# One ring of four PSUM banks for gate, value, attention and W products in a fused attention and SwiGLU kernel

## The chip, the core and the metric

The kernel runs on one core of a Trainium2 chip. The metric is the device time of one execution in microseconds (us). A measurement here can tell two kernels apart when they differ by about 0.2%, which is 1.5 us. In what follows PE is the matrix engine (TensorE), DVE the vector engine, ACT the scalar engine, POOL GpSimd, and SP the engine that issues most DMAs.

## The reference

Eight batches of eight heads with 576 positions of 64 elements go through an attention in two stages: 32 learned queries `p` first gather from all 576 positions, and all positions then attend to these 32 packed rows. The result is the input of a SwiGLU layer of width 512 with a hidden width of 1536.

```python
p_packed = sm_attn(p, k, v)               # (8, 8, 32, 64)
out = sm_attn(q, p_packed, p_packed)      # (8, 8, 576, 64)
x = attn_out.transpose(0, 2, 1, 3).reshape(8 * 576, 512)
g = x @ w_gate                            # 512 x 1536
silu = g * (1.0 / (1.0 + np.exp(-g)))
return silu * (x @ w_val) @ w_out         # 1536 x 512
```

## The kernel before

**What is multiplied.** Since the second attention reads only 32 packed rows for each head, the kernel multiplies these rows with the gate and value weights first: for a batch it forms products M of the packed rows (`ppt`) and the weights (`w_s`), and then multiplies M with the attention weights of the 576 positions (`a2h`, `a2l`). Each operand is kept as a high and a low part, so that a product is three passes: `ml` with `a2h`, `mh` with `a2l`, `mh` with `a2h`.

**Steps.** After a start phase that handles batch 0 (to about 118 us), `batch(1)` follows (118 to 205 us) and then `batch2(b)` for b = 2 to 7. The hidden width is cut into 12 steps, `fc` = 0 to 11. In `batch2` a step is, in the order of PE: chunk A (gate, then value, of 256 or 320 columns: two PSUM banks, called A0 and A1 below, `chunk`, L1248), then `half(0)` (the first half of the products with the output weights for an earlier step, `products`, L1180, in the `acc` banks), chunk B (two banks, B0 and B1), then `half(1)`. ACT reads the gate bank (silu, `sg`, L1254), and DVE then reads the value bank (the product with `sg`, L1261, and for a B chunk a small one into `t`, L1264). Batch 1 has the same chunks in `gv_chunk` (L694, silu L701).

**What runs between the chunks.** After the value matmuls of a chunk a callback `fill` runs with a count that goes from 1 to 8 over the step (two in each chunk, two in each half). At count 2 of each odd step, right behind A1, `m_part` puts two more banks of products on PE, M0 and M1 (32 x 512 each on a part of the array, by a helper, L285 `aux<-w_s,ppt`). ACT rounds them into `mh` (L658), and then DVE makes `ml` (L603), which is the last reader of M0 and M1.

The attention for batch b + 1 is spread over batch b by a table of words, where "1.ha" stands for step 1, in front of `half(0)`. Those that take PSUM banks for PE are `q0` in step 11 of the batch before and `q1` in step 1 (`q_scores`, two banks, L425 `gv_aux<-k_t,p_t`, whose readers are DVE L440 and L441 in `q_read`), `pack` in step 5 (one bank, L509, whose reader is DVE L521 with the result `ppt`), and `mm0` and `mm1` in steps 7 and 9 (two banks each). All of them come right behind A1 or the M products and ahead of `half(0)`. So q0 and q1 stand between A1 and B0 in the order of banks.

In the even batches, step 0 also multiplies the hidden columns that the two batches of a pair share (`p4_step`, six of them, L713 `aux<-t_parts`). All six add into one bank, which `emit_out` copies to `ot` for the DMA to `out` (DVE L193).

**Banks.** Of the eight PSUM banks four are `acc`. Two are `ps_gv`, for the chunks and the attention's scores and packs (`gv_ps`), and two are `ps_aux`, for M and `p4_step` (`ps`). A bank is given again to a later tile when all readers of the tile in it are done, and the first matmul into it waits for that.

**What sets the order.** PE's order is that of the program, by hand. On DVE and ACT a scheduler of the framework orders the instructions, with the attention's kept in program order among themselves (`pin`).

Of the kernel before, what the change touches and what calls it, by code (L numbers as in the profile page):

```python
# [10 lines left out]
F32 = mybir.dt.float32  # L11
# [8 lines left out]
PSUM = bass.MemoryType.PSUM  # L20
# [5 lines left out]
P = 128  # L26
# [107 lines left out]
def tile_pack_attention_swiglu(ctx: ExitStack, tc: tile.TileContext, qT, q0, kT, v, vq, pT, wgv, wout, out):  # L134
# [5 lines left out]
    pool = ctx.enter_context(tc.tile_pool(name="pool", bufs=1))  # L140
    dram = ctx.enter_context(tc.tile_pool(name="dram", bufs=1, space=DRAM))
    ps_acc = ctx.enter_context(tc.tile_pool(name="ps_acc", bufs=4, space=PSUM))
    ps_gv = ctx.enter_context(tc.tile_pool(name="ps_gv", bufs=2, space=PSUM))
    ps_aux = ctx.enter_context(tc.tile_pool(name="ps_aux", bufs=2, space=PSUM))

    early_stack = ExitStack()
    early = early_stack.enter_context(tc.tile_pool(name="early", bufs=1))
# [29 lines left out]
    def pin(ins):  # L177

        return tc.keep_in_program_order(ins) if steady[0] else ins

    def ps():
        turn[0] += 1
        if wide[0] and turn[0] % 2:
            return ps_acc.tile([P, 512], F32, tag="acc", name="acc_aux")
        if wide[0]:
            return ps_gv.tile([P, 512], F32, tag="gv", name="gv_aux")
        return ps_aux.tile([P, 512], F32, tag="aux", name="aux")
# [217 lines left out]
    sq, sc = {}, {}  # L405

    def gv_ps():
        return ps_gv.tile([P, 512], F32, tag="gv", name="gv_aux")

    def q_scores(b, g, bank=ps):  # L410

# [196 lines left out]
    def store_w(k):  # L608
        nc.sync.dma_start(wd[k], w_t[k].rearrange("p h f n -> p (h f n)"))
# [52 lines left out]
    def m_part(b, k, fcs):  # L662
        m_mm(b, k, fcs)
        m_high(b, k, fcs)
# [15 lines left out]
    def gv_chunk(b, fc, is_b, fill, behind, between):  # L680
        odd = b % 2
        n = NB if is_b else NA
        off = (0 if odd else 256) if is_b else (320 if odd else 0)
        mh, ml = ms[b, fc // 2]
        ah, al = a2[b]
        f = fc % 2
        pgs = []
        for s in range(2):
            pg = ps_gv.tile([P, 512], F32, tag="gv", name="gv")
            pgs.append(pg)  # L690
            i = 0
            for m_, a_ in ((ml, ah), (mh, al), (mh, ah)):
                for g in range(NPAR):
                    nc.tensor.matmul(  # L694
                        pg[:, :n], m_[:, g, f, s * P : (s + 1) * P], a_[:, g, off : off + n],
                        start=(i == 0), stop=(i == 5),
                    )
                    i += 1
            fill()
        sg = pool.tile([P, NB], F32, tag="sg", bufs=1, name="sg")  # L700
        nc.scalar.activation(sg[:, :n], pgs[0][:, :n], AF.Silu)  # L701
        behind()
        hf = early.tile([P, 256], F32, tag="hf", bufs=2, name="hf")
        o, o4 = (64, 0) if is_b and odd else (0, 256)
        nc.vector.tensor_tensor(hf, pgs[1][:, o : o + 256], sg[:, o : o + 256], op=ALU.mult)
        if is_b:
            r, r4 = slice(64 * odd, 64 * odd + 64), slice(o4, o4 + 64)
            nc.vector.tensor_tensor(t4[b // 2][:, fc, r], pgs[1][:, r4], sg[:, r4], op=ALU.mult)
        return h_split(hf, nc.scalar, nc.vector, between)
# [82 lines left out]
    with tc.manual_schedule(engines={mybir.EngineType.PE}):  # L792
# [315 lines left out]

        for k in range(NFC // 2):
            store_w(k)  # L1110
        batch(1, behind)
        early_stack.close()
        late = ctx.enter_context(tc.tile_pool(name="late", bufs=1, reuse_waits="tile"))
# [122 lines left out]
        def chunk(b, fc, is_b, fill, behind):  # L1236
            odd = b % 2
            n = NB if is_b else NA
            off = (0 if odd else 256) if is_b else (320 if odd else 0)
            mh, ml = ms[b, fc // 2]  # L1240
            ah, al = a2[b]
            pgs = []
            for s in range(2):
                pg = ps_gv.tile([P, 512], F32, tag="gv", name="gv")
                pgs.append(pg)
                todo = [(m_, a_, g) for m_, a_ in ((ml, ah), (mh, al), (mh, ah)) for g in range(NPAR)]
                for i, (m_, a_, g) in enumerate(todo):
                    nc.tensor.matmul(  # L1248
                        pg[:, :n], m_[:, g, fc % 2, s * P : (s + 1) * P], a_[:, g, off : off + n],
                        start=(i == 0), stop=(i == 5),  # L1250
                    )
                fill()
            sg = pool.tile([P, NB], F32, tag="sg", bufs=1, name="sg")
            nc.scalar.activation(sg[:, :n], pgs[0][:, :n], AF.Silu)  # L1254
            behind()
            at = b, int(is_b), fc // 2
            if fc % 2 == 0:
                raw[at] = places.pop(0)
            x = raw[at][:, fc % 2].rearrange("p t n -> p (t n)")
            o, o4 = (64, 0) if is_b and odd else (0, 256)  # L1260
            nc.vector.tensor_tensor(x, pgs[1][:, o : o + 256], sg[:, o : o + 256], op=ALU.mult)  # L1261
            if is_b:
                r, r4 = slice(64 * odd, 64 * odd + 64), slice(o4, o4 + 64)
                nc.vector.tensor_tensor(t4[b // 2][:, fc, r], pgs[1][:, r4], sg[:, r4], op=ALU.mult)  # L1264

        def batch2(b):
            if not b % 2:
                t4_of(b)
            run = plan_of(b)
            for fc in range(NFC):  # L1270
                t = (b - 2) * NFC + fc
                cur, nxt = pair_at(t), pair_at(t + 1)
                tail = b % 2 == 0 and fc == 0
                count, step = [0], [0]

                def fill():
                    count[0] += 1
                    if count[0] == 2:
                        run(fc, 2)
                        if fc == NFC - 1 and b + 1 < B:  # L1280
                            m_part(b + 1, 0, both)
                            load_ws(b + 1, 1)
                        elif fc % 2 and fc + 1 < NFC:
                            k = (fc + 1) // 2
                            m_part(b, k, both)
                            load_ws(*((b, k + 1) if k < 5 else (b + 1, 0)))
                    else:
                        run(fc, count[0])
                    if tail and count[0] in (1, 3, 4, 5, 6, 8):
                        p4_step(step[0], b - 1)  # L1290
                        step[0] += 1

                def half(which):
                    if cur:
                        products(cur, which, fill)
                    else:
                        fill(), fill()

                chunk(b, fc, False, fill, lambda: run(fc, "a"))
                run(fc, "ha")  # L1300
                if cur:
                    split_sums(cur)
                m_lows()
                half(0)
                if nxt:
                    split_raw(nxt)
                    sum_raw(nxt)
                chunk(b, fc, True, fill, lambda: run(fc, "b"))
                run(fc, "hb")
                half(1)  # L1310
# [56 lines left out]
```

## Time and profile before

| | before |
|---|---|
| median of 3 runs | 752.55 us (752.15 to 753.63) |
| profiled execution, its own time | 754.22 us |
| its span in the trace | 752.4 us |
| mean granted TensorE clock | 0.995 |
| PE busy | 712.0 us (95%) |
| DVE busy | 503.7 us (67%) |
| ACT busy | 403.8 us (54%) |
| POOL busy | 137.6 us (18%) |

The span goes from the first to the last instruction of the trace, and 1.8 us of the profiled execution's time lie around it. Busy time of PE includes the filling of its pipeline, because the ends of matmuls are modelled; a loss of time on PE is better read from the distance between the starts of two instructions. A note in square brackets at a row's end is the idle time ahead of it and what ended that.

### The profile page before, as it was taken

The numbers are of one execution on the slowest core, as the hardware profiler recorded it, in microseconds if no ns is written. First come the engines' busy times: TensorE is split into PE (matmuls) and PEld (weight loads), VectorE is DVE, ScalarE is ACT, GpSimd is POOL, SyncE is SP. The second block draws the span as 40 slices with busy tenths as digits, with TensorE's granted clock in tenths as the row PEclk, the third lists the DMA queues.
The fourth block names the chain that finished last, engine by engine and source line by source line (L and its number), as shares of the span: only waits on it lengthen the run. The fifth ranks groups of instructions, "written<-read, shape, count | busy, mean of one in ns | idle before, by whom it ended". The sixth has DMA issues, their size and how long they took to land.

```text
span 752.4 us, 16344 instructions
## 1 busy us (share of the span) xinstructions
PE 712.0 (95%) x6503; PEld 617.4 (82%) x6503; DVE 503.7 (67%) x1123; ACT 403.8 (54%) x714; POOL 137.6 (18%) x301
## 2 busy tenths in 40 slices
PE   7999988999988998999989999999998999999995
PEld 5777776888876887989879888889887898989985
DVE  4986896767845676677655676676745767646453
ACT  3888455635635465735626357554644546444432
POOL 0000000000010031322303223232311322232331
PEclk9999999999999999999999999999999999999998
DMA  9999953031232433334223342344314322310001
GB/s 356 341 350 349 326 209 124 3 128 64 78 140 91 183 123 128 135 127 166 95 104 120 128 149 111 142 134 144 122 54 155 110 91 113 141 57 29 2 29 42
DMA packets 25436, 103.27 MB, mean 137 GB/s; under 512 B 6672, under 2 KB 7952, under 8 KB 16656
## 3 DMA queue, kind: packets, MB, share of 16 engines
q1 hardware_dynamic: 25072, 102.00, 37.0%
q8 instruction: 51, 0.84, 0.5%
q10 hardware_dynamic: 288, 0.23, 0.1%
q14 instruction: 25, 0.20, 0.1%
HBM read 86.44 MB, written 15.78 MB: 136 GB/s over the span
## 4 chain that ended last, share of the span: by engine, by line
PE 77%; DVE 12%; ACT 5%; issue 2%; DMA 2%; POOL 1%; ACTq 0%; DVEq 0%; SPq 0%; POOLq 0%
PE gv L1248 29%; PE acc L1180 20%; PE acc L713 7%; PE aux L285 6%; PE gv L694 5%; PE gv L944 3%; PE aux L713 3%; DVE ml L603 2%; PE gv_aux L285 1%; DVE ppt L521 1%; DVE ot L1210 1%; ACT mh L658 1%; DMA out<-ot 1%; PE warm_ps L799 1%; ACT sg L1254 1%
## 5 line engine op out<-in xcount | busy, mean ns | idle before, releaser
L1248 PE MATMUL gv<-a2h,ml 128*128 128x256 f32 (+1 forms) x576 | 129.2, 305 | 19.4 <-DVE e L441 8.5
L1248 PE MATMUL gv<-a2l,mh 128*128 128x256 f32 (+1 forms) x576 | 122.1, 293 | 0.0
L1248 PE MATMUL gv<-a2h,mh 128*128 128x256 f32 (+1 forms) x576 | 122.0, 293 | 0.0
L1248 PEld LDWEIGHTS gv<-a2h,ml 128*128 128x128 f32 x576 | 90.0, 188 | 31.0 <-ACT sg L1254 10.5
L1248 PEld LDWEIGHTS gv<-a2l,mh 128*128 128x128 f32 x576 | 91.8, 188 | 0.0
L1248 PEld LDWEIGHTS gv<-a2h,mh 128*128 128x128 f32 x576 | 91.8, 188 | 0.0
L1254 ACT ACTIVATE sg<-gv 128x256 f32<-128x256 f32 (+1 forms) x144 | 59.3, 412 | 51.7 <-PE gv L1248 42.8
L603 DVE TENSOR_TENSOR ml<-aux,mh 128x512 fp32r<-128x512 f32 (+1 forms) x94 | 60.6, 676 | 34.9 <-ACT mh L658 34.8
L1154 ACT CAST hs<-s_raw 128x384 fp32r<-128x384 f32 x72 | 37.0, 514 | 79.3 <-PE acc L1180 76.7
L658 ACT CAST mh<-aux 128x512 fp32r<-128x512 f32 (+1 forms) x94 | 50.0, 584 | 46.9 <-PE aux L285 46.2
L1180 PE MATMUL acc<-wo_h,ho 128*128 128x256 f32 x288 | 66.5, 293 | 2.3 <-DVE ho L1133 2.1
L1180 PEld LDWEIGHTS acc<-wo_h,ho 128*128 128x128 f32 x288 | 49.1, 188 | 18.3 <-issue 14.8
L1180 PE MATMUL acc<-t_w,hs 128*128 128x256 f32 x432 | 62.8, 280 | 0.0
L1180 PE MATMUL acc<-t_w,ho 128*128 128x256 f32 x432 | 62.5, 279 | 0.0
L1180 PEld LDWEIGHTS acc<-t_w,hs 128*128 128x128 f32 x432 | 58.2, 188 | 0.8 <-DVE ot L1210 0.2
L1180 PEld LDWEIGHTS acc<-t_w,ho 128*128 128x128 f32 x432 | 56.1, 188 | 0.2
L1133 DVE TENSOR_TENSOR hs<-s_raw,hs 128x384 fp32r<-128x384 f32 x72 | 39.7, 551 | 21.0 <-ACT hs L1154 20.1
L1139 POOL TENSOR_TENSOR s_raw<-extra 128x128 f32<-128x128 f32 x36 | 16.7, 465 | 196.0 <-DVE hs L1133 177.7
L1261 DVE TENSOR_TENSOR more<-gv,sg 128x256 f32<-128x256 f32 x72 | 30.2, 420 | 27.3 <-PE gv L1248 27.0
L1139 POOL TENSOR_TENSOR s_raw<-more 128x128 f32<-128x128 f32 x36 | 16.6, 462 | 167.3 <-DVE hs L1133 167.3
L1261 DVE TENSOR_TENSOR extra<-gv,sg 128x256 f32<-128x256 f32 x72 | 30.3, 420 | 22.9 <-PE gv L1248 18.9
L285 PE MATMUL aux<-w_s,ppt 64*32 64x512 f32 x576 | 41.3, 601 | 2.3 <-DVE ot L193 2.3
(221 smaller groups left out, 1531.1 us busy)
## 6 DMA issues: line engine op xcount, KB each, us to landing
w_s<-wd SPq DMA_DIRECT2D x36, 1024.0 KB, 5.2
st<-in_wgv SPq DMA_DIRECT2D x12, 1024.0 KB, 7.6
k_t<-in_kT SPq DMA_DIRECT2D x16, 576.0 KB, 4.9
out<-ot SPq DMA_DIRECT2D x35, 256.0 KB, 2.3
q_t<-in_qT SPq DMA_DIRECT2D x14, 576.0 KB, 6.6
v_t<-in_vq SPq DMA_DIRECT2D x6, 1280.0 KB, 8.2
st<-in_wout SPq DMA_DIRECT2D x6, 1024.0 KB, 7.3
wd<-w SPq DMA_DIRECT2D x6, 1024.0 KB, 12.6
```

What stands on the lines that cost most here:

```text
L285: nc.tensor.matmul(outs[par][32 * hp : 32 * hp + 32], lhs(r, hp), rhs(r, hp), start=True, stop=True)
L603: pin(nc.vector.tensor_tensor(*x[1], op=ALU.subtract))
L658: nc.scalar.copy(m[0][at], src)
L694: nc.tensor.matmul(pg[:, :n], m_[:, g, f, s * P : (s + 1) * P], a_[:, g, off : off + n], start=(i == 0), stop=(i == 5),)
L713: nc.tensor.matmul(acc[:, at], h_[:, c : c + P], w_[fc // 2][:, fc % 2, at], start=((fc == 0 or first) and i == 0), stop=(fc == NFC - 1 an ...
L1133: nc.vector.tensor_tensor(dst, src, high.bitcast(F32), op=ALU.subtract)
L1139: nc.gpsimd.tensor_tensor(s_raw[:, 0], a21, a11, op=ALU.subtract)
L1154: nc.scalar.copy(hi, s_raw)
L1180: nc.tensor.matmul(acc[bank][:, QC * col : QC * col + QC], h_[:, x], w_, start=(k == 0 and i == 0 and col == 0), stop=(k == 5 and i == 2 a ...
L1248: nc.tensor.matmul(pg[:, :n], m_[:, g, fc % 2, s * P : (s + 1) * P], a_[:, g, off : off + n], start=(i == 0), stop=(i == 5),)
L1254: nc.scalar.activation(sg[:, :n], pgs[0][:, :n], AF.Silu)
L1261: nc.vector.tensor_tensor(x, pgs[1][:, o : o + 256], sg[:, o : o + 256], op=ALU.mult)
```

## The change

The pools `ps_gv` and `ps_aux` are closed after the start phase, and one pool of four banks takes their place from `batch(1)` on. The chunks, the attention's tiles, M and `p4_step` all take the next bank of it in program order. Where nothing holds a bank for long, a tile follows the one four allocations back. `p4_step` holds its bank over step 0 and a part of step 1 of an even batch, and there the other three rotate. The six steps of `p4_step` stand at counts 2 to 7 rather than 1, 3, 4, 5, 6 and 8.

```diff
-    ps_gv = ctx.enter_context(tc.tile_pool(name="ps_gv", bufs=2, space=PSUM))
-    ps_aux = ctx.enter_context(tc.tile_pool(name="ps_aux", bufs=2, space=PSUM))
+    narrow_stack = ExitStack()
+    ps_gv = narrow_stack.enter_context(tc.tile_pool(name="ps_gv", bufs=2, space=PSUM))
+    ps_aux = narrow_stack.enter_context(tc.tile_pool(name="ps_aux", bufs=2, space=PSUM))
+    ring = []
...
+    def ring_ps(name):
+        return ring[0].tile([P, 512], F32, tag="ring", name=name)
+
     def ps():
+        if ring:
+            return ring_ps("aux")
...
     def gv_ps():
-        return ps_gv.tile([P, 512], F32, tag="gv", name="gv_aux")
+        return ring_ps("gv_aux") if ring else ps_gv.tile([P, 512], F32, tag="gv", name="gv_aux")
...
-            pg = ps_gv.tile([P, 512], F32, tag="gv", name="gv")
+            pg = ring_ps("gv")
...
+        narrow_stack.close()
+        ring.append(ctx.enter_context(tc.tile_pool(name="ps_ring", bufs=4, space=PSUM, reuse_waits="tile")))
         batch(1, behind)
...
-                pg = ps_gv.tile([P, 512], F32, tag="gv", name="gv")
+                pg = ring_ps("gv")
...
-                    if tail and count[0] in (1, 3, 4, 5, 6, 8):
+                    if tail and 1 < count[0] < 8:
```

The lines of the changed kernel lie 7 further down from L425 on (L432), and 9 from L1180 on (L1189). PE's instructions are the same, and one of the `p4_step` moves in each of the batches 2, 4 and 6 from between A0 and A1 to behind A1. On ACT eight instructions change places and on DVE 21, with none added; what changes at most places is only which bank is waited for.

Step 11 of batch 4, in PE's order before. A0 and A1 are `gv_5600` and `gv_5610`, M0 and M1 `aux_5619` and `aux_5620`, the two banks of q0 `gv_aux_5639` and `gv_aux_5640`, B0 and B1 `gv_5685` and `gv_5692`.

```order
L1248 MATMUL gv_5600<-a2h_4063,ml_5441 128x256 [waits Activation_49]
...
L1248 MATMUL gv_5610<-a2h_4063,ml_5441 128x256 [waits DVE_49,PE_49]
...
L285 MATMUL aux_5619<-w_s_5454,ppt_5106 32x512 [waits DMAHW3_49]
L285 MATMUL aux_5620<-w_s_5454,ppt_5106 32x512
...
L425 MATMUL gv_aux_5639<-k_t_4952,p_t_4950 32x144 [waits DMAHW4_49,Activation_49]
L425 MATMUL gv_aux_5640<-k_t_4952,p_t_4950 32x144 [waits DVE_49]
...
L1248 MATMUL gv_5685<-a2h_4063,ml_5441 128x320 [waits DVE_49,PE_49]
...
L1248 MATMUL gv_5692<-a2h_4063,ml_5441 128x320 [waits Activation_49]
```

The two banks of the chunks go round as A0, A1, q0, q0, B0, B1, so B0 comes into the bank that q0's first tile has just filled, and B1 into the one of the second. The same place after the change, with A0 and A1 as `gv_5605` and `gv_5615`:

```order
L1257 MATMUL gv_5605<-a2h_4068,ml_5446 128x256 [waits Activation_49]
...
L1257 MATMUL gv_5615<-a2h_4068,ml_5446 128x256 [waits DVE_49]
...
L292 MATMUL aux_5624<-w_s_5459,ppt_5111 32x512 [waits DMAHW3_49,Activation_49]
L292 MATMUL aux_5625<-w_s_5459,ppt_5111 32x512 [waits DVE_49,PE_49]
...
L432 MATMUL gv_aux_5644<-k_t_4957,p_t_4955 32x144 [waits DMAHW4_49,Activation_49]
L432 MATMUL gv_aux_5645<-k_t_4957,p_t_4955 32x144 [waits DVE_49]
...
L1257 MATMUL gv_5690<-a2h_4068,ml_5446 128x320 [waits DVE_49]
...
L1257 MATMUL gv_5697<-a2h_4068,ml_5446 128x320 [waits DVE_49]
```

The four banks go round as A0, A1, M0, M1, then q0 in those of A0 and A1, and B0 and B1 in those of M0 and M1. B0 and B1 now wait for DVE's `ml` of M0 and M1.

Step 1 of batch 4, in PE's order before, where M0 and M1 are `aux_4692` and `aux_4693`, the tiles of q1 `gv_aux_4709` and `gv_aux_4710`, B0 and B1 `gv_4759` and `gv_4766`:

```order
L285 MATMUL aux_4692<-w_s_4461,ppt_3936 32x512 [waits DMAHW0_49]
L285 MATMUL aux_4693<-w_s_4461,ppt_3936 32x512 [waits DVE_49]
...
L425 MATMUL gv_aux_4709<-k_t_3782,p_t_3780 32x144 [waits Activation_49]
L425 MATMUL gv_aux_4710<-k_t_3782,p_t_3780 32x144
...
L1248 MATMUL gv_4759<-a2h_4063,ml_4448 128x320 [waits DVE_49,PE_49]
...
L1248 MATMUL gv_4766<-a2h_4063,ml_4448 128x320 [waits Activation_49]
```

And after, the same tiles as `aux_4697`, `aux_4698`, `gv_aux_4714`, `gv_aux_4715`, `gv_4764` and `gv_4771`:

```order
L292 MATMUL aux_4697<-w_s_4466,ppt_3941 32x512 [waits DMAHW0_49,DVE_49,PE_49]
L292 MATMUL aux_4698<-w_s_4466,ppt_3941 32x512 [waits Activation_49]
...
L432 MATMUL gv_aux_4714<-k_t_3787,p_t_3785 32x144 [waits DVE_49]
L432 MATMUL gv_aux_4715<-k_t_3787,p_t_3785 32x144 [waits DVE_49]
...
L1257 MATMUL gv_4764<-a2h_4068,ml_4453 128x320 [waits DVE_49]
...
L1257 MATMUL gv_4771<-a2h_4068,ml_4453 128x320 [waits DVE_49]
```

Before, M1 came into the bank of `p4_step`, and its first matmul waited for DVE's copy of that bank (L193). After, `p4_step` still holds a bank here, so three rotate: M1 comes into A0's bank, q1's first tile into A1's, its second into M0's, B0 into M1's. The wait of `gv_aux_4715` is for DVE's `ml` of M0.

DVE's order at the same place, before (`ot_4665<-aux_4552` is the copy of `p4_step`'s bank, `extra` the product of A1):

```order
L1261 TENSOR_TENSOR extra_2495<-gv_4683,sg_4706 128x256 [waits PE_49,Activation_49]
L193 COPY ot_4665<-aux_4552 128x512 [waits DMAHW1_49,DVE_49]
L603 TENSOR_TENSOR ml_4691<-aux_4692,mh_4690 128x512 [waits Activation_49]
L603 TENSOR_TENSOR ml_4691<-aux_4693,mh_4690 128x512 [waits Activation_49]
L440 TENSOR_REDUCE z1_4467<-gv_aux_4709 128x2 [waits PE_49]
```

And after:

```order
L1270 TENSOR_TENSOR extra_2500<-gv_4688,sg_4711 128x256 [waits PE_49,Activation_49]
L610 TENSOR_TENSOR ml_4696<-aux_4697,mh_4695 128x512 [waits Activation_49]
L610 TENSOR_TENSOR ml_4696<-aux_4698,mh_4695 128x512 [waits Activation_49]
L200 COPY ot_4664<-aux_4564 128x512 [waits DMAHW1_49,DVE_49]
L447 TENSOR_REDUCE z1_4472<-gv_aux_4714 128x2 [waits PE_49]
```

The copy with its wait for a DMA has moved behind the two `ml`.

## Rows read from the trace of the kernel before

**Rows 1.** The page's busy times, and its groups by line (part 5)

```profile
PE 712.0 (95%) x6503; PEld 617.4 (82%) x6503; DVE 503.7 (67%) x1123; ACT 403.8 (54%) x714; POOL 137.6 (18%) x301
...
L1248 PE MATMUL gv<-a2h,ml 128*128 128x256 f32 (+1 forms) x576 | 129.2, 305 | 19.4 <-DVE e L441 8.5
...
L1248 PE MATMUL gv<-a2h,mh 128*128 128x256 f32 (+1 forms) x576 | 122.0, 293 | 0.0
```

**Rows 2.** Busy time by stretch, batch 5: length, PE, PEld, DVE, ACT, POOL, clock, DMA, GB/s

```profile
464.00:555.00 91.00, 87.43 (x854) 78.51 (x854) 62.75 (x145) 53.75 (x91) 24.95 (x53) 1.00 0.35 124
```

**Rows 3.** Waits of PE from 160 us on: total us, times, longest us

```profile
PE gv L1248 <- DVE e L441: 8.5, 9, 2.8
PE gv L1248 <- ACT sg L1254: 7.5, 11, 1.6
PE aux L285 <- DVE ot L193: 2.3, 2, 1.2
...
PE gv L1248 <- DVE ppt L521: 1.5, 4, 0.4
```

**Rows 4.** Timeline of PE around step 11 of batch 4 (start, length)

```profile
458.89 1.09 PE L285 MATMUL aux<-w_s,ppt 64*32 64x512 f32 x16
...
460.45 0.39 PE L1180 MATMUL acc<-wo_h,ho 128*128 128x256 f32 x1
...
461.28 0.86 PE L1180 MATMUL acc<-t_w,ho 128*128 128x256 f32 x6
462.98 0.53 PE L1248 MATMUL gv<-a2h,ml 128*128 128x320 f32 x2 [0.84 <-DVE e L441]
...
464.69 0.57 PE L1248 MATMUL gv<-a2h,ml 128*128 128x320 f32 x2 [0.59 <-ACT sg L1254]
...
465.69 0.86 PE L1180 MATMUL acc<-t_w,hs 128*128 128x256 f32 x6
...
468.81 0.87 PE L1180 MATMUL acc<-t_w,ho 128*128 128x256 f32 x6
...
471.27 0.87 PE L1180 MATMUL acc<-t_w,hs 128*128 128x256 f32 x6
```

**Rows 5.** Timeline of DVE at the same place

```profile
460.69 1.29 DVE L603 TENSOR_TENSOR ml<-aux,mh 128x512 fp32r<-128x512 f32 x2 [1.20 <-ACT mh L658]
```

**Rows 6.** Timeline of PE, step 1 of batch 4

```profile
387.35 1.04 PE L285 MATMUL aux<-w_s,ppt 64*32 64x512 f32 x2
...
391.09 0.39 PE L1180 MATMUL acc<-wo_h,ho 128*128 128x256 f32 x1
...
396.25 0.87 PE L1180 MATMUL acc<-t_w,hs 128*128 128x256 f32 x6
```

**Rows 7.** Timeline of DVE, step 1 of batch 4

```profile
388.80 0.69 DVE L193 COPY ot<-aux 128x512 f32<-128x512 f32 x1 [0.84 <-DMA out<-ot]
```

**Rows 8.** Timeline of PE, step 1 of batch 5

```profile
476.71 0.86 PE L1180 MATMUL acc<-t_w,ho 128*128 128x256 f32 x6
...
480.52 0.75 PE L1180 MATMUL acc<-t_w,hs 128*128 128x256 f32 x5
```

**Rows 9.** Timeline of PE in batch 1 (step 11) and batch 2 (steps 1, 2 and 5)

```profile
195.10 0.50 PE L694 MATMUL gv<-a2h,ml 128*128 128x256 f32 x2 [0.36 <-ACT sg L701]
...
223.35 0.54 PE L1248 MATMUL gv<-a2h,ml 128*128 128x320 f32 x2 [2.78 <-DVE e L441]
...
230.43 0.51 PE L1248 MATMUL gv<-a2h,ml 128*128 128x256 f32 x2 [1.56 <-ACT sg L1254]
...
243.42 0.77 PE L509 MATMUL gv_aux<-v_t,a 128*32 128x64 f32 x40
```

**Rows 10.** Timeline of SP in batch 2: the issue of the gather of q's sums

```profile
230.85 1.75 SPq L460 DMA_DIRECT2D x<-zd  x4
```

**Rows 11.** Busy time by stretch in batch 1: columns as in rows 2

```profile
126.00:130.00 4.00, 1.75 (x9) 1.07 (x7) 3.50 (x7) 2.92 (x5) 0.00 (x0) 1.00 0.94 308
130.00:134.00 4.00, 3.89 (x12) 3.42 (x13) 3.48 (x9) 1.54 (x3) 0.00 (x0) 0.57 0.03 9
```

## The prediction

> **What bounds the kernel now.** I read the page's busy times first. PE is busy for 712.0 of 752.4 us, DVE for 503.7 and ACT for 403.8 [rows 1], so PE sets the pace and the other two can only hurt it through waits. The table by stretches says the same of a single batch: in the 91 us of batch 5, PE has 87.43, DVE 62.75 (69%), ACT 53.75 (59%), and the clock is at 1.00, the upper of its two levels [rows 2]. Gains can only come from the places where PE waits, so the next view is the table of PE's waits from 160 us on [rows 3]. Its two large rows are chunk matmuls that wait for DVE L441, the last reader of the q scores (8.5 us, nine times), and for the silu on ACT (7.5 us, eleven times). These are waits for a bank, since a chunk's matmuls need nothing else from these two instructions.
>
> The timeline then shows what one of them costs [rows 4]. Behind the products of `half(0)`, whose last group starts at 461.28, B0 starts only at 462.98 (idle 0.84 for DVE L441), B1 at 464.69 (idle 0.59 for the silu), and the next products at 465.69. That is 4.41 us. One step later, with nothing between A1 and B0, the same stretch goes from 468.81 to 471.27, which is 2.46. So 1.95 us are lost where the two notes add up to 1.43. I take losses from start to start, and where I have only the idle notes I multiply by 1.95 / 1.43 = 1.36.
>
> **The change part by part.** No instruction is added or taken away, so every term is a wait that goes, stays or comes.
>
> *q0 in step 11 of batches 2 to 5.* B0 waits there for the reader of q0's bank, and B1 for the silu of B0, because only two banks go round. After the change both wait for the `ml` of M0 and M1 [rows 5]: two of them from 460.69, 1.29 long together, so the first ends at about 461.33 and the second at 461.98. B0 cannot come before the products end, at 461.28 + 0.86 = 462.14, and B1 comes after B0. B0 has 0.8 us to spare. The whole loss goes: 4 x 1.95 = **7.8**.
>
> *q1 in step 1 of batches 3 and 5.* From 476.71 to 480.52 are 3.81 us [rows 8], less 2.46 gives 1.35; 2 x 1.35 = **2.7**.
>
> *q1 in step 1 of batches 4 and 6.* Three things happen here. M1 waits before for the bank of `p4_step`, whose copy on DVE starts at 388.80 because it waits for the output DMA before it [rows 7]; M and q1 take 391.09 - 387.35 = 3.74 us [rows 6], against 460.45 - 458.89 = 1.56 undisturbed [rows 4], so 2.18 are lost, and they go, since M1 comes into A0's bank. The chunk B behind loses what it loses at q0: 396.25 - 391.09 = 5.16 [rows 6] against 465.69 - 460.45 = 5.24 [rows 4], so 1.95 - 0.08 = 1.87 go. A new wait comes: only three banks rotate here, and the second tile of q1 waits for the `ml` of M0. No row shows that wait. From the start of M to the end of the first `ml` are 461.33 - 458.89 = 2.44 us [rows 4, 5], and q1 would be due half way through M and q1, after 0.78, so it costs 1.66. Its bounds are zero (if M's readers are on time for some other reason) and the 3.74 of today. What is queued on PE behind it is q1 and then `half(0)`; the copy with its DMA wait now stands behind both `ml` on DVE and holds up only q1's readers, which are not waited for by PE until much later. Net 2.18 + 1.87 - 1.66 = 2.4 for each; 2 x 2.4 = **4.8**.
>
> *The pack in step 5 of batches 3 to 6.* B1 waits four times for DVE L521, 1.5 us in all [rows 3]; x 1.36 = **2.0**. In a ring of four, B1 does not come into the pack's bank.
>
> *Batches 1 and 2.* In batch 1 the silu wait of 0.36 at 195.10 [rows 9] goes: x 1.36 = **0.5**. Of the 7.5 us of silu waits [rows 3] the four at q0 (0.59 each) and four at q1 (taken alike) make at most 4.7, so three more share about 3.0, and the largest of them, 1.56 at 230.43, is in batch 2 [rows 9]. x 1.36 = 4.1. But the softmax chain of batch 2 begins with a gather by DMA issued at 230.85 [rows 10], and the pack at 243.42 [rows 9] needs its end. What PE wins ahead of the pack it can lose again in front of it, since that chain gets no faster. Between 0 and 4.1 I take **2.6**. The longest wait of all, 2.78 at 223.35 [rows 9], stays: B0 gets the bank of q1 there in the new order too.
>
> *Small waits everywhere.* Of three passes with the same shape and count, the first, which begins each chunk, has 129.2 us and the last 122.0 [rows 1]. These 7.2 us are mostly first matmuls that start late by 0.1 to 0.4 us for a silu or a product two chunks back. With four banks they wait for one that is four tiles back. Some of the 7.2 belongs to the stalls above. Between 2 and 7.2 I take **5.0**.
>
> Sum: 7.8 + 2.7 + 4.8 + 2.0 + 0.5 + 2.6 + 5.0 = 25.4. I take off 2 us, with bounds of 0 and 4, because DVE and ACT do the same work in less time: a batch that loses 5 of its 91 us has DVE at 73% and ACT at 63%, and somewhere an `ml` or a product will come late for a bank. The profiled execution took 754.22 us, 0.2% above the median of 752.55, and its stalls are those of every execution, so I take the gain from the median: 752.5 - 23.4 = 729.
>
> **A rule that speaks against it.** The granted clock was 1.00 through batch 5 with all the waits named above [rows 2]. It fell once near here, to 0.57 over 130 to 134 us, between its two levels of 2.4 and 1.2 GHz, after a stretch in which PE was busy for 1.75 of 4 us [rows 11]; that cost 4 x (1 - 0.57) = 1.7 us. If short waits at the banks brought such a dip at each of the 13 attention places above (four q0, four q1, four packs, one in batch 1), 13 x 1.7 = 22 us would be lost. The Trainium skill ("TensorE: Matmul & The Clock Gate", section "A second HAM failure mode: psum-queue depth-cycling") tells of a kernel that cycles through PSUM banks in each iteration, in which PE idles so often for a moment between groups of matmuls that the clock swings between its levels. By that page the ring itself could cost the gain; this trace has PE cycling through banks now, with longer idle moments than the ring would leave, and the clock stays up.
>
> **The rivals.**
>
> 1. *The waits go, as summed.* With the bounds: 25.4 + 2.2 (small waits at 7.2) + 1.5 (batch 2 at 4.1) gives 29.1, or 723.5 us; 25.4 - 3.0 - 2.6 - 4.0 gives 15.8, or 736.7. Chance 0.70.
>
> 2. *DVE takes half of it back.* In the ring M's `ml` is in every rotation of an odd step: there are 25 places (five attention words in each of five batches) at which an attention tile or B0 or B1 follows M0 or M1 into a bank. B0 has 0.8 us to spare at q0. If one product and one `ml` of other work came ahead of it, 1.3 us [rows 5], 0.5 would be lost at each: 25 x 0.5 = 12.5, and 752.5 - 25.4 + 12.5 = 740. For it speaks that DVE stands at 69%; against it that the order on DVE hardly changes and `ml` comes 0.8 us ahead of need. Chance 0.19.
>
> 3. *Slower: the M products couple with the attention.* What I found for q1 in batches 4 and 6, the second tile waiting 1.66 us for the `ml` of M0, could hold at all 25 places, if in fact only three banks rotated or if a bank held long broke the rotation. That is 23 more: 23 x 1.66 = 38, and 752.5 - 25.4 + 38 = 765. It loses from 25.4 / 1.66 = 15 more places on. The order shows this wait at two places; at step 11 the second tile of q0 waits for A1's product, as before. Chance 0.06.
>
> 4. *The change does little*, because the pool hands out the banks that were waited for before, as it does at 223.35: 752. The order shows otherwise at q0 and q1 of batch 4. Chance 0.03.
>
> 5. *The clock*, by the dips above: 752.5 - 25.4 + 22 = 749. Chance 0.02.
>
> **The numbers.** The likeliest is the first, 729, with a range of its own from 723.5 to 737. Reaching to the second case on the slow side and a little beyond the bounds on the fast side gives 722 to 742. What a measurement of this kernel can tell from no change is about 0.2%, 1.5 us. Faster by more than that are the cases 1, 2 and 5: 0.91. Within it case 4: 0.03. Slower case 3: 0.06.
>
> **What would show it.** In the changed profile the waits of chunk matmuls for the q scores' subtraction should be down to about 2.8 us, one time, and those for the silu to under 2; the pack's wait and the copy's wait should be gone from PE. In step 11 the stretch of 4.41 us should read about 2.5, in step 1 of batch 4 the q1 tiles should show a wait for `ml` of about 1.7. The first-pass group should come within 2 to 3 us of the last. The batches 3 to 6 should each be shorter by some 4 to 6 us, batch 2 by about 5. I am wrong if PE waits for `ml` at more than those two places or if the chunks' second matmuls start to wait for DVE's products, and wrong in the other direction if batch 2's chain also moves forward and gives its full 4 us.

## The result and the profile after

The changed kernel takes 730.11 us (median of four runs, 727.82 to 733.33) against 753.09 us of the kernel before, which now has four runs as well: a ratio of 0.9696 with a 95% interval of 0.9654 to 0.9738, or 23 us less. The forecast was 729, with a range from 722 to 742.

The page of the changed kernel has these lines in place of [rows 1], busy times first and then the groups of PE that begin and end a chunk:

```profile
PE 700.8 (96%) x6503; PEld 612.2 (84%) x6503; DVE 502.2 (69%) x1123; ACT 403.6 (55%) x714; POOL 138.1 (19%) x301
...
L1257 PE MATMUL gv<-a2h,ml 128*128 128x256 f32 (+1 forms) x576 | 123.3, 295 | 3.7 <-DVE e L448 2.8
...
L1257 PE MATMUL gv<-a2h,mh 128*128 128x256 f32 (+1 forms) x576 | 121.7, 292 | 0.0
```

The counts of instructions on every engine are what they were. What is gone is idle time of PE ahead of the first pass, 19.4 us before and 3.7 now, and most of the extra length of that pass, 129.2 - 122.0 = 7.2 us before and 123.3 - 121.7 = 1.6 now.

The table of PE's waits from 160 us on, in place of [rows 3]:

```profile
PE gv L1257 <- DVE e L448: 2.8, 1, 2.8
...
PE aux L292 <- DVE t L1273: 1.8, 1, 1.8
PE gv_aux L432 <- DVE ml L610: 1.4, 2, 0.7
PE gv_aux L432 <- DVE extra L1270: 1.2, 4, 0.4
PE gv L1257 <- ACT sg L1263: 0.5, 1, 0.5
```

Of the chunks' waits for the q scores one is left of nine, of those for the silu one of eleven, and PE has none for the pack or for the copy. Two waits of q tiles for `ml` have come, as forecast. The wait of 1.8 us of M for `t` was not forecast, and with it the clock fell, which the part on batch 2 comes back to.

Step 11 of batch 4 on PE, in place of [rows 4]:

```profile
445.69 1.09 PE L292 MATMUL aux<-w_s,ppt 64*32 64x512 f32 x16
...
448.07 0.86 PE L1189 MATMUL acc<-t_w,ho 128*128 128x256 f32 x6
448.78 0.45 PE L1257 MATMUL gv<-a2h,ml 128*128 128x320 f32 x2
...
449.66 0.46 PE L1257 MATMUL gv<-a2h,ml 128*128 128x320 f32 x2
...
450.54 0.86 PE L1189 MATMUL acc<-t_w,hs 128*128 128x256 f32 x6
```

and DVE there, in place of [rows 5]:

```profile
447.48 1.29 DVE L610 TENSOR_TENSOR ml<-aux,mh 128x512 fp32r<-128x512 f32 x2 [1.06 <-ACT mh L665]
```

From 448.07 to 450.54 are 2.47 us, where it was 4.41: B0 and B1 start one behind the other with no idle note. Taken as half of the two, the first `ml` ends at about 447.48 + 0.64 = 448.12, 0.66 us ahead of B0 (its own record in the trace ends at 448.18, so 0.60), and the second at 448.77, 0.89 ahead of B1.

Step 1 of batch 4 on PE, in place of [rows 6]:

```profile
378.53 1.09 PE L292 MATMUL aux<-w_s,ppt 64*32 64x512 f32 x16
379.97 0.43 PE L432 MATMUL gv_aux<-k_t,p_t 64*32 64x144 f32 x2 [0.35 <-DVE extra L1270]
381.07 0.72 PE L432 MATMUL gv_aux<-k_t,p_t 64*32 64x144 f32 x30 [0.68 <-DVE ml L610]
381.72 0.39 PE L1189 MATMUL acc<-wo_h,ho 128*128 128x256 f32 x1
...
385.01 0.75 PE L1189 MATMUL acc<-t_w,hs 128*128 128x256 f32 x5
```

M no longer waits for the copy, and the second tile of q1 waits for `ml` of M0. From M to the products behind chunk B are 385.01 - 378.53 = 6.48 us, against 396.25 - 387.35 = 8.90 in [rows 6]: 2.42 won, 2.4 forecast.

Where the time went from stretch to stretch is read by laying the same PE instruction of the two traces side by side. Each row is a chunk matmul that begins A0 of some step, with its start before and after:

| stretch that ends at this start | before | after | distance | won in the stretch |
|---|---|---|---|---|
| start phase | 118.80 | 118.99 | +0.19 | -0.2 |
| batch 1 | 206.03 | 204.58 | -1.45 | 1.6 |
| batch 2 | 290.36 | 286.78 | -3.58 | 2.1 |
| batch 3 | 371.89 | 363.11 | -8.78 | 5.2 |
| batch 4 | 466.74 | 451.59 | -15.15 | 6.4 |
| batch 5 | 551.04 | 530.72 | -20.32 | 5.2 |
| batch 6 | 648.99 | 624.23 | -24.76 | 4.4 |

Behind it the distance stays, and the spans are 752.4 and 727.7.

### The profile page after: what moved, and what is told of

Same layout as the page of the kernel before. It is cut to its first block, busy times and chain, and to the rows that moved or that the text cites. A ratio compares the mean times of both kernels' runs of the same rounds, so it can differ in the third digit from the quotient of the medians.

```text
span 727.7 us, 16349 instructions
## 1 busy us (share of the span) xinstructions
PE 700.8 (96%) x6503; PEld 612.2 (84%) x6503; DVE 502.2 (69%) x1123; ACT 403.6 (55%) x714; POOL 138.1 (19%) x301
## 4 chain that ended last, share of the span: by engine, by line
PE 82%; DVE 9%; ACT 4%; issue 3%; DMA 1%; POOL 1%; ACTq 0%; DVEq 0%; SPq 0%; POOLq 0%
PE gv L1257 29%; PE acc L1189 23%; PE acc L720 7%; PE aux L292 6%; PE gv L701 5%; PE aux L720 4%; PE gv L951 3%; PE gv_aux L292 1%; PE gv_aux L516 1%; PE warm_ps L806 1%; PE gv_aux L432 1%; DMA st<-in_wout 1%; DVE ml L610 1%; DVE hs L1142 1%; DVE ot L1219 1%
## 5 line engine op out<-in xcount | busy, mean ns | idle before, releaser
L1257 PE MATMUL gv<-a2h,ml 128*128 128x256 f32 (+1 forms) x576 | 123.3, 295 | 3.7 <-DVE e L448 2.8
L1257 PE MATMUL gv<-a2l,mh 128*128 128x256 f32 (+1 forms) x576 | 121.7, 292 | 0.0
L1257 PE MATMUL gv<-a2h,mh 128*128 128x256 f32 (+1 forms) x576 | 121.7, 292 | 0.0
L1189 PE MATMUL acc<-wo_h,ho 128*128 128x256 f32 x288 | 66.5, 293 | 2.3 <-DVE ho L1142 2.1
L1189 PEld LDWEIGHTS acc<-wo_h,ho 128*128 128x128 f32 x288 | 49.1, 188 | 18.4 <-issue 14.8
L1189 PE MATMUL acc<-t_w,hs 128*128 128x256 f32 x432 | 63.1, 280 | 0.0
L1189 PE MATMUL acc<-t_w,ho 128*128 128x256 f32 x432 | 62.5, 279 | 0.0
L1189 PEld LDWEIGHTS acc<-t_w,hs 128*128 128x128 f32 x432 | 58.6, 188 | 0.9 <-DVE ot L1219 0.2
L1189 PEld LDWEIGHTS acc<-t_w,ho 128*128 128x128 f32 x432 | 56.1, 188 | 0.2
L292 PE MATMUL aux<-w_s,ppt 64*32 64x512 f32 x576 | 41.5, 607 | 2.3 <-DVE t L1273 1.8
L1189 PE MATMUL acc<-wo_l,ho 128*128 128x256 f32 x144 | 40.8, 283 | 0.0
```

What stands on the lines that cost most here:

```text
L292: nc.tensor.matmul(outs[par][32 * hp : 32 * hp + 32], lhs(r, hp), rhs(r, hp), start=True, stop=True)
L1189: nc.tensor.matmul(acc[bank][:, QC * col : QC * col + QC], h_[:, x], w_, start=(k == 0 and i == 0 and col == 0), stop=(k == 5 and i == 2 a ...
L1257: nc.tensor.matmul(pg[:, :n], m_[:, g, fc % 2, s * P : (s + 1) * P], a_[:, g, off : off + n], start=(i == 0), stop=(i == 5),)
```

## The experiments

**The ring from batch 3 on.** Batches 1 and 2 keep the four narrow banks.

```diff
-        narrow_stack.close()
-        ring.append(ctx.enter_context(tc.tile_pool(name="ps_ring", bufs=4, space=PSUM, reuse_waits="tile")))
         batch(1, behind)
...
         for b in range(2, B):
+            if b == 3:
+                narrow_stack.close()
+                ring.append(ctx.enter_context(tc.tile_pool(name="ps_ring", bufs=4, space=PSUM, reuse_waits="tile")))
             batch2(b)
```

> The ring of four starts at batch 3 instead of batch 1; batches 1 and 2 keep the two pools of two. Theory A (the gain is the sum of bank waits behind q0, q1 and the packs plus small ones, and batch 2 keeps nothing because its softmax chain holds the pack): the distance between the traces of before and after grew by 4.5, 7.0, 5.2 and 4.4 us over the batches 3 to 6, 21.1 in all, so about 732 us, 1 to 3 us above the changed kernel, and the pack of step 5 in batch 2 no more than 1 us away from where it is in the kernel before. Rival B (batches 1 and 2 give what the prediction gave them, 0.5 + 2.6 + 1.95 and a fifth of the small waits): 6 us above the changed kernel, 736.

Measured: 732.88 us, 2.8 above the changed kernel (ratio to before 0.972, 0.9688 to 0.9751). Theory A. By the table, batches 3 to 6 carry 21 of the 23 us, and the other two little. The 2.8 us by themselves are within the noise, since the two intervals overlap.

**Three banks.** The same, with `bufs=3`, and from batch 3 on `m_lows()` stands ahead of `run(fc, "ha")`, so that the reads of q come behind `ml` in DVE's program.

```diff
+                if b > 2:
+                    m_lows()
                 run(fc, "ha")
```

> As the ring from batch 3, but of three banks, and with the ml of M ahead of the attention's reads in the program. Theory A: with three banks the second tile of q0, q1, mm0 and mm1 follows M0, as at q1 of batches 4 and 6 now, where M and q1 take 3.19 us against 1.56. That is 15 places from batch 3 on, two of which pay it already: 13 x 1.63 = 21 us more, about 754. Rival C (DVE is early enough, and three banks do as well as four): under 740.

Measured: 753.72 us in one run, 20.8 above the ring of four from batch 3. The sum is theory A's, to the microsecond. PE's waits from 290 us on in that trace:

```profile
PE gv_aux L432 <- DVE ml L610: 8.0, 7, 1.4
PE gv_aux L292 <- DVE ml L610: 5.8, 8, 1.0
```

Seven pairs of q and eight of the second attention (`gv_aux L292`) wait for `ml`, 15 places as counted. Place by place it is not what was counted, and the exact sum is luck: laid beside the ring of four from batch 3, seven places lose 1.63 to 1.69 us from M's start to the products of `half(0)`, six only 1.0 to 1.1, and the two q1 in batches 4 and 6, counted as paid already, 2.0 more each. The chunks and the products take as long as with four banks, so moving `m_lows()` cost PE nothing there. With one bank less the ring gives back all that the ring of four won over those batches.

**Chunks apart from the rest.** Two banks for the chunks, two for M, the attention and `p4_step`, from batch 3 on, and `m_lows()` ahead of `run(fc, "ha")` as with three banks.

```diff
+                for n in ("ps_chunk", "ps_rest"):
+                    ring.append(ctx.enter_context(tc.tile_pool(name=n, bufs=2, space=PSUM, reuse_waits="tile")))
...
-        return ring[0].tile([P, 512], F32, tag="ring", name=name)
+        return ring[name != "gv"].tile([P, 512], F32, tag="ring", name=name)
```

> From batch 3 on no ring: two banks for the chunks alone, and two that M, the attention and the shared columns' products share. B0 and B1 then never wait for the attention. Theory A (what counts is which tile follows which): every attention tile follows M0 or M1, the second of a pair waits to the end of the second ml, some 2.3 us at 15 places, and the single tile of a pack 1.7 at four: 41 us, and the small waits between chunks stay, 5: about 778. Rival D (it is enough to take the attention out of the chunks' banks): about 737.

Measured: 795.06 us in one run, 62 above the ring of four from batch 3, where theory A had 46 and D had 5. PE's waits:

```profile
PE gv_aux L292 <- DVE ml L610: 11.6, 8, 1.5
PE gv_aux L432 <- DVE ml L610: 11.0, 12, 1.5
PE gv_aux L516 <- DVE ml L610: 5.8, 4, 1.5
PE aux L292 <- DVE ot L200: 5.2, 2, 2.6
```

Now the attention's tiles wait for `ml`. Laid beside the ring of four, the first tile of a pair, counted from M's start, came 1.66 us later in the trace at 13 places and each pack 1.52: 13 x 1.66 + 4 x 1.52 = 28. At the other two pairs, q1 in batches 4 and 6, M1 waits for the copy of `p4_step`'s bank again, and the first tile came 4.7 and 5.6 us later, 10.3. The chunks, products and second tiles together took 23 us longer, and much of that is the clock, by the table of stretches (length, then busy time of PE, PEld, DVE, ACT, POOL, then the granted clock):

```profile
300.00:500.00 200.00, 182.22 (x1671) 159.13 (x1670) 124.39 (x282) 98.11 (x168) 45.96 (x98) 0.96 0.32 116
500.00:700.00 200.00, 185.28 (x1645) 163.21 (x1644) 123.13 (x278) 98.02 (x171) 47.50 (x101) 0.95 0.30 106
```

and around the first of the two waits for the copy:

```profile
396.00:400.00 4.00, 1.74 (x9) 0.71 (x8) 2.51 (x7) 0.39 (x2) 1.82 (x4) 1.00 0.35 131
400.00:404.00 4.00, 2.24 (x39) 0.86 (x46) 1.56 (x3) 1.07 (x2) 0.00 (x0) 0.80 0.47 162
404.00:408.00 4.00, 4.00 (x37) 3.56 (x23) 1.74 (x4) 0.40 (x1) 0.00 (x0) 0.50 0.89 336
```

PE was busy for 1.74 and 2.24 of 4 us, and then ran at 0.50, the lower level, while busy all the time. 200 x 0.04 + 200 x 0.05 = 18 us is an upper estimate of what the clock took. 28 + 10 + 23 = 61 covers the 62; how the clock and small waits share the 23 was not measured. Theory A had named the waits for `ml`, 28 us here where it had 41, but neither the copy nor the clock.

**`ml` twice.** How much DVE has to spare.

```diff
-            pin(nc.vector.tensor_tensor(*x[1], op=ALU.subtract))
+            for _ in range(1 + bool(ring)):
+                pin(nc.vector.tensor_tensor(*x[1], op=ALU.subtract))
```

> The changed kernel, with each ml subtraction of M on DVE done twice from batch 1 on (the second writes the same values), 0.64 us more before each of M's banks comes free, 1.29 before the second. Theory A (B0 has 0.66 us and B1 0.89 to spare at step 11): B0 just makes it, B1 is 0.4 us late at 14 pair places, and q1 of batches 4 and 6 pay 0.6 to 1.3 more: 5 to 10 us slower, about 738. Rival E (DVE is the next bound, as the second case of the prediction had it): every doubled subtraction shows at all 25 places, 1.29 each, 32 us slower, about 762.

Measured: 752.86 us, 23 above the changed kernel (ratio to before 0.998, 0.996 to 0.9999). Neither theory: A said 5 to 10, E said 32. Read against the changed kernel's trace, 11.4 of the 23 us come in batches 1 and 2 and 11.0 in batches 3 to 6. PE's waits from 118 to 290 us, where both batches lie:

```profile
PE gv L1258 <- DVE ml L611: 4.9, 5, 1.3
...
PE gv L702 <- DVE ml L611: 2.5, 4, 1.1
```

I had counted the places of the later batches. In the two early batches chunks also wait for `ml`, at nine places. The clock has a part in the 11.4 too: it was 0.76, 0.50 and 0.89 over the three stretches of 4 us from 226 on and 0.67 and 0.50 over the two from 254 on, at most 4 x 1.68 = 6.7 us, against at most 1.7 in the changed kernel's batch 2. So the doubling was tried from batch 3 on alone:

> The changed kernel with the ml of M done twice from batch 3 on only. Theory A, revised (the 23 us of the run with all of them doubled are 11.4 in batches 1 and 2, where DVE has long queues, and 11.0 in batches 3 to 6, where B0 and B1 come 0.4 to 0.5 us late and q1 of batches 4 and 6 0.8): 741. Rival E (DVE is full everywhere, and delay is handed on from batch to batch): most of the 23 us show again, 748 or more.

Measured: 743.19 us, 13 above the changed kernel. Theory A, revised, which had 741. In the trace two falls of the clock at q1 in batches 4 and 6 are part of it (0.65 over 384 to 388 us, 0.67 over 560 to 564). The slack read at step 11, 0.6 and 0.9 us, is not that of every place. At `mm1` in step 9 the attention's reads stand between the two `ml`, and in batch 3 of the changed kernel the second `ml` and then B1 read

```profile
347.45 0.65 DVE L610 TENSOR_TENSOR ml<-aux,mh 128x512 fp32r<-128x512 f32 x1
```

```profile
348.18 0.45 PE L1257 MATMUL gv<-a2h,ml 128*128 128x320 f32 x2
```

So B1 has 348.18 - 348.10 = 0.08 us to spare there, and the same in batches 4 to 6: the ring just holds.

**The moved steps alone, and the ring without them.** The last line of the diff by itself in the kernel before, and the changed kernel with that line undone.

```diff
-                    if tail and count[0] in (1, 3, 4, 5, 6, 8):
+                    if tail and 1 < count[0] < 8:
```

> The kernel before, with only the six shared-column steps at counts 2 to 7; no ring. Theory A (the gain is the ring's alone; side by side the moved steps cost 0.7 us on PE at one place and give it back at the next): 753, within 1.5 us of the kernel before. Rival F (the move gives part of the gain, since a step no longer stands between A0 and A1): 2 to 5 us faster, 748 to 751.

> The changed kernel with the shared-column steps back at counts 1, 3, 4, 5, 6 and 8. Theory A: within 2 us of the changed kernel, 730. Rival F (the ring needs the move, since the held bank else falls between A0 and A1): 2 to 5 us slower, 732 to 735.

Measured: alone 757.24 us (ratio to before 1.0035, 1.0018 to 1.0052), slower, against both theories. Undone 729.74 us (0.9675, 0.9657 to 0.9692), no different from the changed kernel, as theory A had it. The gain is the ring's. Why the move alone costs is seen at M1 in batch 4, on PE in that trace:

```profile
385.17 1.04 PE L285 MATMUL aux<-w_s,ppt 64*32 64x512 f32 x2
388.80 0.66 PE L285 MATMUL aux<-w_s,ppt 64*32 64x512 f32 x7 [2.58 <-DVE ot L193]
```

The wait for the copy, 1.15 us before the move, is 2.58 now, and 5.2 for 2.3 over its two places. In the ring M does not follow that bank, so it does not matter there.

**Batch 2: the pack later.** In batch 2 alone "5.ha pack" becomes "6.ha pack".

> The changed kernel with the pack of batch 2 alone one step later, in step 6 instead of 5. Theory A (PE ran ahead by 4.4 us in batch 2 up to step 5 and gave all of it back at M and the pack there, waiting for a softmax chain that did not get faster): the chain is done by then, and 2 to 4 us come back, 726 to 728. Rival G (something else in batch 2 limits, the ml for the next chunk or the tiles of step 7): the wait turns up one step later, 730.

Measured: 730.07 us, as the changed kernel. Theory A fell: PE was not held by the softmax's result. (That profile has a fall of the clock which the changed kernel's has not, to 0.67 over 222 to 226 us, ahead of the pack, and it cost 1.3 us, so the equal times alone would not rule a small gain out; the wait that stayed does.) The wait of 1.8 us of M1 for `t` stood in that trace as in the changed kernel's, where PE and DVE read

```profile
237.39 1.04 PE L292 MATMUL aux<-w_s,ppt 64*32 64x512 f32 x2
240.23 1.60 PE L292 MATMUL aux<-w_s,ppt 64*32 64x512 f32 x14 [1.80 <-DVE t L1273]
```

```profile
236.74 1.43 DVE L501 TENSOR_TENSOR e<-e,y 128x576 f32<-128x576 f32 x2
238.08 1.56 DVE L504 STREAM_TRANSPOSE a<-e 128x640 f32<-128x640 f32 x2
239.57 0.38 DVE L1270 TENSOR_TENSOR more<-gv,sg 128x256 f32<-128x256 f32 x1
239.88 0.20 DVE L1273 TENSOR_TENSOR t<-gv,sg 128x64 f32<-128x64 f32 x1
```

M1 follows chunk B's value bank in the ring, and the last reader of that bank stands on DVE behind 3 us of scaling and transposing for the softmax.

**Batch 2: the softmax's last words later.** So those were moved behind the products, with the pack still in step 6:

```diff
-        return FIRST if d == 2 else LATER
+        return FIRST if d == 2 else LATER.replace("3.7 load_k turn0", "3.7 load_k").replace("4.ha turn1", "4.hb turn0").replace("5.ha pack", "5.ha turn1\n    6.ha pack") if d == 3 else LATER
```

> The changed kernel with, in batch 2 alone, the last two words of the softmax (scaling and transposes on DVE) behind chunk B of step 4 and of step 5's chunk A, and the pack in step 6 as in the run before. Theory A, revised (M1 of step 5 follows chunk B's value bank in the ring, and its last reader, the product into t, stood on DVE behind 3 us of scaling and transposing; the pack had nothing to do with it): the wait of 1.8 us for t is gone from PE and 2 to 4 us come back, 726 to 728. Rival G (the chain only gets later and PE waits for it at the pack or at the attention tiles of step 7): 729 to 731.

Measured: 727.64 us (0.9653, 0.9624 to 0.9682). In the trace batch 2 is 2.7 us shorter than in the changed kernel, the clock stays at 1.00 over 238 to 246 us, and M runs in one piece:

```profile
237.97 1.77 PE L292 MATMUL aux<-w_s,ppt 64*32 64x512 f32 x16
```

Theory A, revised.

**`p4_step` early.** Six steps in the first half of step 0, so that the bank is free before step 1.

```diff
-                    if tail and 1 < count[0] < 8:
+                    for _ in range((0, 0, 2, 2, 2)[count[0]] if tail and count[0] < 5 else 0):
                         p4_step(step[0], b - 1)
```

> The changed kernel with the six shared-column steps two at a time at counts 2, 3 and 4, so that their bank is copied out before the products' results take the two output buffers, and four banks rotate again at q1 of batches 4 and 6. Theory A (there the second tile of q1 pays 1.63 us for the ml of M0, and the first about 0.35 for A1's product behind other DVE work): 3 to 4 us faster, about 726.5. Rival H (steps in pairs wait for their high and low parts from ACT and DVE, up to 0.8 us at four of them in three batches): the gain is lost, 730 or more.

Measured: 726.61 us (0.9663, 0.9615 to 0.9711). q1 in step 1 of batch 4, on PE:

```profile
377.95 1.09 PE L292 MATMUL aux<-w_s,ppt 64*32 64x512 f32 x16
378.83 0.75 PE L432 MATMUL gv_aux<-k_t,p_t 64*32 64x144 f32 x32
379.51 0.39 PE L1189 MATMUL acc<-wo_h,ho 128*128 128x256 f32 x1
```

From M's start to the products of `half(0)` are 379.51 - 377.95 = 1.56 us, 1.63 less than in the changed kernel's trace, where 381.72 - 378.53 = 3.19. Theory A; 1.3 us stay at each of the two places, since chunk B behind q1 takes a little longer there. The steps in pairs lose next to nothing.

**Both.** The last two edits together.

> The two edits together that touch what the ring leaves: the shared-column steps early and batch 2's softmax words later. Theory A, revised (the two waits lie in different batches and add up): 3 us from the first and 2 to 4 from the second, 723 to 725. Rival (the second brings nothing): 726.6, as the first alone.

Measured: 723.69 us (723.60 to 724.75, ratio to before 0.9603, 0.9577 to 0.9628), the fastest version of this study, some 6 us under the changed kernel. Theory A, revised. Its batch 2 has no fall of the clock and is 3.7 us shorter than the changed kernel's. PE is busy for 97% of the span, and its waits from 160 us on are

```profile
PE gv L1257 <- DVE e L448: 2.8, 1, 2.8
PE acc L1189 <- DVE ho L1142: 2.1, 2, 1.4
PE gv L1257 <- DVE ml L610: 0.8, 1, 0.8
```

## Why the prediction was right, point by point

**q0, 7.8 us.** Right in mechanism and size: 4.41 - 2.47 = 1.94 in batch 4, 1.95 forecast, and 1.92 to 1.93 at the other three places. The readers that B0 and B1 now follow come some 0.6 and 0.9 us ahead of need.

**q1, 2.7 and 4.8 us.** Right: 1.35 at each place in batches 3 and 5, and 2.42 at each in batches 4 and 6, new wait included. The price of that wait, which no row had shown and which was taken at 1.66 from [rows 4, 5], is 3.19 - 1.56 = 1.63, although the idle note shows only 0.68 of it. `p4_step` early takes it away, and with three banks seven more places have it in full.

**Packs, 2.0 us.** In batch 5 the stretch around chunk B, before and then after, is

```profile
504.97 0.87 PE L1180 MATMUL acc<-t_w,ho 128*128 128x256 f32 x6
...
508.05 0.86 PE L1180 MATMUL acc<-t_w,hs 128*128 128x256 f32 x6
```

```profile
487.77 0.87 PE L1189 MATMUL acc<-t_w,ho 128*128 128x256 f32 x6
...
490.23 0.87 PE L1189 MATMUL acc<-t_w,hs 128*128 128x256 f32 x6
```

These are 3.08 and 2.46 us: 0.62 won here and 0.59 to 0.61 at the other three, 2.4. Right, a little small.

**Small waits, 5.0 us.** The table of stretches gives batches 3 to 6 21.2 us. Taking off q0 (3 x 1.94), q1 (2.7 + 2 x 2.42) and the packs (2.4) leaves 5.4 for them in these four batches. That is what is left over and not a measurement of each wait; 1.7 of it is seen at chunk B of step 4, which went from 2.9 to 2.46 us in each of the four. The first pass lost 7.2 - 1.6 = 5.6 of its extra length over all, stalls of the other terms included. Right as far as this shows.

**Batch 2, 2.6 us.** This term was mis-sized. Batch 2 won 2.1 in all, where about 5 were named, and 1.9 of them are its q0, so its early stalls gave about 0.2, not 2.6. PE did win them, 3.6 us by step 5, since the waits for the silu went, and then gave back 4.4 at M and the pack there. The prediction had named the place and put it down to the DMA gather and its chain. The runs showed another cause: the pack alone one step later changed nothing (730.07), and the softmax's words behind chunk B's products brought 727.64. It is a wait of the ring itself, M1 for a value bank whose reader is late on DVE. Behind this wait the clock fell, in the changed kernel's profile as follows:

```profile
238.00:242.00 4.00, 2.20 (x28) 0.45 (x30) 2.51 (x6) 0.53 (x2) 0.00 (x0) 0.83 0.00 0
242.00:246.00 4.00, 3.47 (x88) 3.04 (x81) 1.72 (x8) 1.37 (x3) 0.00 (x0) 0.74 0.71 262
```

That took at most 4 x 0.17 + 4 x 0.26 = 1.7 us of the 4.4. The pack, which lies in this stretch, took 2.36 us, as here, against 1.32 in the kernel before:

```profile
241.76 2.36 PE L516 MATMUL gv_aux<-v_t,a 128*32 128x64 f32 x80
```

All five profiles with this wait (the changed kernel's, the pack later, `p4_step` early, the steps not moved, `ml` twice from batch 3 on) have a fall behind it, and the two with the softmax's words moved, which have no such wait, have 1.00 over these 8 us. So what the moved words brought is the wait and the clock together.

**Batch 1, 0.5 us.** This term was too large as well. 1.6 us were won in the profiled executions, but nearly all of it is luck. The clock that fell to 0.57 in 130 to 134 us before [rows 11] did not fall in the changed kernel's profile:

```profile
126.00:130.00 4.00, 1.94 (x10) 1.22 (x8) 3.31 (x6) 2.92 (x5) 0.00 (x0) 1.00 0.89 301
130.00:134.00 4.00, 3.70 (x24) 3.48 (x25) 3.96 (x11) 2.14 (x5) 0.00 (x0) 1.00 0.06 17
```

A chunk that starts at 130.33 before and 130.52 after is followed by one at 134.01 and 132.63: the distance between the traces grew by 1.57 us just there. The kernel with the moved steps alone runs the same program as the kernel before in batch 1, and there the clock stayed up too:

```profile
126.00:130.00 4.00, 1.65 (x10) 1.42 (x10) 3.97 (x8) 2.92 (x4) 0.00 (x0) 1.00 0.77 293
130.00:134.00 4.00, 4.00 (x27) 3.60 (x26) 3.66 (x11) 2.11 (x5) 0.00 (x0) 1.00 0.02 4
```

Its batch 1 took 85.75 us by the rows of the table, the changed kernel's 85.59, so the change won 0.16. Of the 24.7 us between the two spans 23.1 are then the change's, in line with the medians' 23.0.

**Take-back, 2 us.** Nothing was taken back in batches 3 to 6. What was taken back, was in batch 2. The two terms together counted 2.6 - 2.0 = 0.6, and 0.2 came, so the sum held although the place of the loss was not foreseen. That these two errors, the small waits' free choice within its bounds and the packs' and batch 1's small misses came out within 1 us of the forecast is partly luck.

**The rivals.** The second (DVE takes half back at 25 places) did not come, but it was near: for B0 and B1 DVE was in time at every place from batch 3 on, by 0.08 us only at step 9. Twice the `ml` from batch 3 on costs 13 us; that this is near the 12.5 priced for other places and delays is chance. The third (M couples with the attention) would have been real with one bank less: 753.72, no gain at all. The forecast for 25 places was 765, and from batch 3 on there were 15, none of them packs. The fourth (the same banks handed out again) holds at the one place it was seen at, the wait of 2.8 us that stayed. The fifth (the clock) did not come at its 13 places, and the mean clock was 0.996 in the profiled execution with the ring; what came is one fall, behind M1's wait in batch 2. The Trainium skill ("TensorE: Matmul & The Clock Gate", section "A second HAM failure mode: psum-queue depth-cycling") tells of a kernel that cycles through banks in each iteration, in which PE idles so often for a moment that the clock swings. Here the ring of four cycles through more banks than each of the two pools before and left the clock up through its batches but for that fall, and it fell more than once in the version with two pools of two, where PE idled most. That fits idle time and not the cycling as what matters, but it is not shown: the version with three banks, whose PE waits 8.0 + 5.8 = 13.8 us for `ml`, ran at 0.998.

One difference was not tried by itself: the new pool has `reuse_waits="tile"`, which the two old ones lack. Three banks and two pools of two have it too and lose the gain, so it does not bring the gain alone; no run has four banks without it.

## What to carry to other kernels

When banks are shared in a ring, ask of each tile which tile's bank it follows and on what queue that tile's last reader stands: four banks won 23 us, and three, or two and two, lost it all, because a tile then followed one whose reader needed two engines in turn (with two and two the clock added to it). A tile that holds a bank for long shortens the ring for everybody, so let it go before the crowded step. And where a gain vanishes within a batch, move the reader that is waited for, not the wait's neighbour; the chain that looks guilty by time may only stand beside it.

## What was not expected of the hardware

The clock fell in one profiled execution of the kernel before, to 0.57 after 1.75 busy us of 4 [rows 11]. At the same place it stayed at 1.00 after 1.94 of 4 in the changed kernel's, and after 1.65 of 4 in that of the kernel with the moved steps, which is the same program up to there. A dip of some 1.6 us can thus come or stay away between executions of the same work, a little more or less busy time did not tell which, and a comparison of two single profiles carries it.
